# Weight preparations of the gate stage: one tile to load into and another to store from, sums made in place, and a new timetable

## The chip, the cores and the metric

The kernel runs on one core of a Trainium2 chip. The metric is device time in microseconds (us) of the whole program, so lower is better. Engines are named as the profile names them: PE is TensorE's matmul and PEld its weight load, DVE is VectorE, ACT is ScalarE, POOL is GpSimd, SP is SyncE, which does nothing here but issue DMAs. Each engine works through its own queue in order, and an instruction that waits holds what stands behind it on that queue.

## The reference, cut to what matters

The input is layer-normalised; a Fourier mixing layer and a gated feed-forward layer work on the same normalised x, and both are added to the residual.

```python
xn = _layernorm(x)                                   # x: 2048 x 640
a  = einsum("bsd,ed->bse", xn, dft_hid_re)
b  = einsum("bsd,ed->bse", xn, dft_hid_im)
yA = einsum("ts,bse->bte", dft_seq_re, a) - einsum("ts,bse->bte", dft_seq_im, b)
gate = einsum("bsd,df->bsf", xn, W_gate)             # 640 x 1728
up   = einsum("bsd,df->bsf", xn, W_up)
h    = gate * (gate > 0) * up
yB   = einsum("bsf,fd->bsd", h, W_down)              # 1728 x 640
return x + yA + yB
```

The kernel orders the matrix products another way (the sequence transform of xn first, then the product with the hidden matrices together with W_down) and writes them as Winograd-like block products: sums and differences of blocks stand in for some of the multiplications. Each fp32 product is three matmuls of rounded high and low parts, which the helper `mm3` issues on lines 205 to 207.

## The kernel before, in words

There are three stages. The first streams the sequence matrix and normalises x. The second, the **gate stage**, makes the gate and up products for 13 tiles of 128 columns. The third, `project`, multiplies everything by the hidden matrices and W_down.

The gate stage has a timetable written out by hand. Every action is filed under a key with `at(key, function)`; the list is sorted by key, and the instructions of all engines are issued in that order. A tile takes `PERIOD = 33` keys. In a whole-numbered key stands one block product, which is three matmuls on PE; other work has fractional keys between them. `STEPS` holds the products (`mm`), the copies that seed a new PSUM bank from an old one (`seed`, line 1094, on ACT), snapshots (`snap`, line 196) and sums (`add`, line 1104; `addout`, line 1109; both on DVE). `SUMS` lists differences of weight blocks on line 999, which `plan_sums` puts on DVE or on POOL by their due keys. `WEIGHTS` are the roundings of weights to high parts on ACT (line 196) and low parts on DVE (line 1075).

Beside the gate products, the stage also prepares weights that the third stage needs. There are 29 **preparations**, numbered here from 0: five of `quad_weights`, then 24 of `pair_half`. Three stand in each tile from the third tile on, at the keys in `TASK_KEYS`. A preparation has five steps, each filed under its own key:

- `load`, `TASK_LEAD` keys ahead: two DMAs on SP's queue (line 1256 or 1292) into a tile `pw`
- `prepare`: three or four sums of 128x128 blocks on DVE (lines 1263 to 1266, or 1298 and on with the helper on line 625)
- `round_`, 1.2 keys later: one rounding on ACT (line 1270 or 1305)
- `rounded`, at the second number of the pair in `TASK_KEYS`: the low part on DVE (line 1274 or 1309)
- `store`, `TASK_STORE` keys after that: one or two DMAs on SP (lines 1278 and 1280, or 1312) to the DRAM tensors `wparts` or `wquads`

The pool `prep` has two buffers, each 12 blocks wide. A `pw` tile holds what is loaded, what is computed and what is stored, so the load of preparation i writes into the tile of preparation i-2 and waits on SP until the store of i-2 has landed. SP's queue also carries the results of the gate products (`hd`, line 1130) and the next tile's raw weights (lines 986, 991, 996). POOL's queue has DMAs of its own, the sums of data for the third stage (`grown`, lines 1338 and 1339) and unchanged weight blocks (line 1241).

`rest_weights` takes a tile of the same pool ahead of the gate stage, and `lead_unit` takes some at its end.

Of the kernel before, what the change touches and what calls it, by code (L numbers as in the profile page):

```python
# [127 lines left out]
def fnet_reglu_kernel(  # L128
# [877 lines left out]
    def plan_sums():  # L1006

        split_at = {b: key for key, src, first, k, _ in WEIGHTS if src == "z" for b in range(first, first + k)}
        reads = {}
        for i, (_, o, _, a, b) in enumerate(SUMS):  # L1010
            for x in (a, b):
                reads.setdefault(x, []).append(i)
        made = {o: i for i, (_, o, *_) in enumerate(SUMS)}
        due = {}

        def due_at(i):
            if i not in due:
                o = SUMS[i][1]
                raw = max(SUMS[i][3:]) >= ZR
                due[i] = min([split_at.get(o, 99.0) - 9, RAW_DUE if raw else 99.0] + [due_at(j) - 0.8 for j in reads.get(o, ())])  # L1020
# [133 lines left out]
    def rest_weights():  # L1154
        st = stage()[:, :D]
        nc.sync.dma_start(st, wrest)
        rest["w"] = w = pool("prep").tile([P, 12 * P], F32R, name="pw")[:, : 2 * D].rearrange("p (v d) -> p v d", v=2)
        split(w[:, 0], w[:, 1], st)

    def rest_block(i, k):  # L1160
        ks = sorted(range(KD), key=lambda k: block(k, CHUNKS[i]) in late_raw)
        return block(ks[k], CHUNKS[i])

    def rest_multiply(i, k):
        d = rest_block(i, k) // NT
        w, cs = rest["w"], slice(d * P, (d + 1) * P)
        if k == 0:
            rest[i] = new_bank()
        mm3(rest[i], (w[:, 0, cs], w[:, 1, cs]), place[rest_block(i, k)], k == 0, k == KD - 1)
# [74 lines left out]
    def pair_half(k, h):  # L1244

        t = {}
        z1, z4, y11, y12, y21 = (slice(i * P, (i + 1) * P) for i in range(5))
        hi, lo = slice(5 * P, 8 * P), slice(8 * P, 11 * P)
        z2, z3, y22 = (slice(i * P, (i + 1) * P) for i in (8, 9, 10))

        def load():
            t["z"] = z = pool("prep").tile([P, 12 * P], F32, name="pw")
            wa, wb = pair(k, 1)
            blocks = z.rearrange("p (o n) -> p o n", n=P)
            for w, put in ((wa[0], slice(2, 5, 2)), (wb[0], slice(3, 11, 7))):
                nc.sync.dma_start(blocks[: w.shape[0], put], w.rearrange("p (o n) -> p o n", n=P)[:, h : h + 4 : 3])

        def prepare():
            z = t["z"]
            if k == ODD:  # L1260
                nc.vector.memset(z[REST:, y12], 0.0)
                nc.vector.memset(z[REST:, y22], 0.0)
            tt(z[:, z1], z[:, y21], z[:, y22], op=OP.add)
            blocks = z.rearrange("p (o n) -> p o n", n=P)
            tt(blocks[:, 8:10], blocks[:, 0:3:2], blocks[:, 2:5:2], op=OP.subtract)
            tt(z[:, z4], z[:, y12], z[:, z2], op=OP.subtract)

        def round_():
            z = t["z"]
            nc.scalar.activation(z[:, hi].bitcast(F32R), z[:, lo], AF.Copy)  # L1270

        def rounded():
            z = t["z"]
            tt(z[:, lo], z[:, lo], z[:, hi], op=OP.subtract)

        def store():
            z = t["z"]
            nc.sync.dma_start(wparts[:, k, : 10 * P].rearrange("p (a n) -> p a n", a=2)[:, :, h * P : (h + 1) * P],
                                z[:, : 2 * P].rearrange("p (a n) -> p a n", a=2))
            nc.sync.dma_start(wparts[:, k, HIGH:NW].rearrange("p (v n) -> p v n", n=2 * P)[:, :, h * P : (h + 1) * P],  # L1280
                                z[:, 5 * P : 11 * P].rearrange("p (v n) -> p v n", n=P))

        return load, prepare, round_, rounded, store

    def quad_weights(i):

        t = {}

        def load():
            t["z"] = z = pool("prep").tile([P, 12 * P], F32, name="pw")  # L1290
            for j, k in enumerate(QUADS[i]):
                nc.sync.dma_start(z[:, j * 2 * P : (j + 1) * 2 * P], pair(k, 1)[1][0][:, : 2 * P])

        def prepare():
            a11, a21, a12, a22 = (t["z"][:, j * P : (j + 1) * P] for j in range(4))
            t["s"] = s = t["z"][:, 4 * P : 12 * P].rearrange("p (s v n) -> p s v n", s=4, v=2)
            s1, s2, s3, s4 = (s[:, j, 1] for j in range(4))
            tt(s1, a22, a21, op=OP.subtract)
            minus(s2, s1, a11)
            tt(s3, a11, a21, op=OP.subtract)  # L1300
            minus(s4, a12, s2)

        def round_():
            s = t["s"]
            nc.scalar.activation(s[:, :, 0].bitcast(F32R), s[:, :, 1], AF.Copy)

        def rounded():
            s = t["s"]
            tt(s[:, :, 1], s[:, :, 1], s[:, :, 0], op=OP.subtract)

        def store():
            nc.sync.dma_start(wquads[:, i], t["s"].rearrange("p s v n -> p s (v n)"))

        return load, prepare, round_, rounded, store
# [33 lines left out]
    def lead_unit(u):  # L1348
# [439 lines left out]
```

## Time and profile before

| | us |
|---|---|
| median of 3 runs | 1016.29 |
| lowest and highest run | 1012.73, 1021.4 |
| the profiled execution's own time | 1020.64 |
| its span, first to last instruction | 1018.8 |
| PE busy | 999.3 (98%) |
| DVE busy | 882.7 (87%) |
| ACT busy | 525.0 (52%) |
| POOL busy | 146.0 (14%) |

The profiled execution is one run by itself. Its time is 1.84 us more than its span, and 4.35 us above the median of the three timed runs. The gate stage lies from about 398 to 740 us of the span. Waits are read as "engine, instruction, releaser: us in total, times, longest"; in a timeline the first two numbers are an instruction's start and duration, and the bracket at the end is the idle time of its engine ahead of it and what ended that.

### The profile page before, as it was taken

Reading aid. Unit: us, or ns where it says so; the run is one execution under the profiler, and the core shown is the slowest. Engines: PE = TensorE matmul, PEld = TensorE weight load, DVE = VectorE, ACT = ScalarE, POOL = GpSimd, SP = SyncE. Lnnn points to the kernel's source line nnn. Section 1 sums busy time; section 2 is a strip of 40 time slices with the busy share of each in tenths; the row PEclk is TensorE's granted clock in tenths of the full one; section 3 lists DMA queues with packets and bytes.
Section 4 is the critical chain, followed back from the end, with each engine's and each line's share of the span. In section 5 each row is a group of like instructions: output and inputs, shape, how many; then the busy total and the mean of one; then the engine's idle time right before and its main releaser. Section 6 shows DMA issues by size and latency. Waiting matters only on the chain.

```text
span 1018.8 us, 13540 instructions
## 1 busy us (share of the span) xinstructions
PE 999.3 (98%) x4393; PEld 820.8 (81%) x4393; DVE 882.7 (87%) x1440; ACT 525.0 (52%) x832; POOL 146.0 (14%) x285
## 2 busy tenths in 40 slices
PE   9999999999999999999899899999999999999998
PEld 7888888888888888778688678888877888888887
DVE  7968999999989989989799689997778888589877
ACT  6664443433333556776476466666434454444542
POOL 2000000000000000034344344432000001000001
PEclk9999999999999999999899989999999999999999
DMA  9877894977939867547687888866599779999785
GB/s 333 328 231 278 265 341 141 388 266 233 374 126 333 297 216 267 196 133 196 211 259 225 232 230 237 220 195 177 183 388 322 228 249 330 317 300 341 223 259 184
DMA packets 183669, 261.12 MB, mean 256 GB/s; under 512 B 14944, under 2 KB 127200, under 8 KB 183504
## 3 DMA queue, kind: packets, MB, share of 16 engines
q1 hardware_dynamic: 147200, 208.82, 60.7%
q0 software_dynamic: 10944, 38.44, 12.9%
q10 hardware_dynamic: 25456, 13.01, 4.3%
q8 instruction: 34, 0.56, 0.2%
q14 instruction: 35, 0.29, 0.1%
HBM read 198.34 MB, written 75.94 MB: 269 GB/s over the span
## 4 chain that ended last, share of the span: by engine, by line
PE 84%; DMA 6%; DVE 6%; ACT 2%; issue 1%; SPq 0%; POOL 0%; DVEq 0%; ACTq 0%
PE ps L205 26%; PE ps L206 26%; PE ps L207 26%; PE ps L583 3%; DMA wparts<-pw 2%; DMA wquads<-pw 1%; DMA rw<-pq 1%; DVE gw L999 1%; PE ps L612 1%; DMA pw<-in_wd 1%; DMA rw<-hd 1%; DVE w L1075 1%; DMA wt<-wparts 1%; PE ps L1587 1%; DVE ev L1109 1%
## 5 line engine op out<-in xcount | busy, mean ns | idle before, releaser
L206 PE MATMUL ps<-cb,wt 128*128 128x512 f32 (+1 forms) x389 | 151.5, 390 | 1.3 <-DVE cb L200 1.2
L205 PE MATMUL ps<-cb,wt 128*128 128x512 f32 (+1 forms) x389 | 151.1, 388 | 0.4 <-ACT cb L199 0.4
L207 PE MATMUL ps<-cb,wt 128*128 128x512 f32 (+1 forms) x389 | 150.9, 388 | 0.0
L199 ACT ACTIVATE cb<-rw 128x1024 fp32r<-128x1024 f32 (+1 forms) x91 | 86.6, 962 | 77.4 <-PE ps L207 39.8
L199 ACT ACTIVATE cb<-raw 128x1024 fp32r<-128x1024 f32 x64 | 67.7, 1060 | 103.3 <-PE ps L207 70.8
L200 DVE TENSOR_TENSOR cb<-rw,cb 128x1024 fp32r<-128x1024 f32 (+1 forms) x91 | 99.4, 1103 | 18.2 <-ACT cb L199 17.6
L206 PE MATMUL ps<-cb,xs_late 128*128 128x512 f32 x232 | 90.5, 390 | 0.0
L207 PE MATMUL ps<-cb,xs_late 128*128 128x512 f32 x232 | 90.3, 389 | 0.0
L205 PE MATMUL ps<-cb,xs_late 128*128 128x512 f32 x232 | 90.3, 389 | 0.0
L196 ACT ACTIVATE ev<-ps 128x512 f32<-128x512 f32 x117 | 69.7, 596 | 38.3 <-PE ps L207 36.4
L200 DVE TENSOR_TENSOR cb<-raw,cb 128x1024 fp32r<-128x1024 f32 x64 | 77.9, 1218 | 13.1 <-ACT cb L199 13.0
L1094 ACT ACTIVATE ps<-ps 128x512 f32<-128x512 f32 x104 | 59.3, 582 | 58.0 <-DVE ps L1104 36.9
L206 PE MATMUL ps<-cb,xs_early 128*128 128x512 f32 x226 | 88.0, 390 | 0.0
L205 PE MATMUL ps<-cb,xs_early 128*128 128x512 f32 x226 | 87.9, 389 | 0.0
L207 PE MATMUL ps<-cb,xs_early 128*128 128x512 f32 x226 | 87.9, 389 | 0.0
L206 PEld LDWEIGHTS ps<-cb,wt 128*128 128x128 f32 x389 | 73.0, 188 | 18.3 <-DVE cb L200 3.3
L205 PEld LDWEIGHTS ps<-cb,wt 128*128 128x128 f32 x389 | 73.0, 188 | 15.8 <-ACT cb L199 0.8
L207 PEld LDWEIGHTS ps<-cb,wt 128*128 128x128 f32 x389 | 73.0, 188 | 14.9
L1109 DVE TENSOR_TENSOR ev<-ps,ev 128x512 f32<-128x512 f32 x91 | 62.4, 686 | 13.0 <-PE ps L207 12.0
L199 ACT ACTIVATE wt<-wt 128x768 fp32r<-128x768 f32 (+5 forms) x60 | 38.4, 646 | 56.6 <-DMA wt<-wparts 54.9
L999 POOL TENSOR_TENSOR gw<-gw 128x128 f32<-128x128 f32 x99 | 45.9, 463 | 149.6 <-DVE gw L999 62.2
L205 PE MATMUL ps<-mv,w 128*128 128x512 f32 x143 | 57.1, 399 | 5.6 <-ACT ps L1094 5.6
(250 smaller groups left out, 2290.4 us busy)
## 6 DMA issues: line engine op xcount, KB each, us to landing
raw<-in_dft SPq DMA_DIRECT2D x94, 512.0 KB, 6.5
wt<-wparts SPq DMA_DIRECT2D x74, 256.0 KB, 4.9
rw<-hd SPq DMA_DIRECT2D x27, 512.0 KB, 6.7
hd<-ev SPq DMA_DIRECT2D x45, 256.0 KB, 3.1
tok<-r ACTq DMA_DIRECT2D x24, 448.0 KB, 6.0
wt<-wparts SPq DMA_DIRECT2D x27, 384.0 KB, 5.0
rw<-pq SPq DMA_DIRECT2D x19, 512.0 KB, 5.8
wparts<-pw SPq DMA_DIRECT2D x24, 384.0 KB, 4.2
```

What stands on the lines that cost most here:

```text
L196: return nc.scalar.activation(o, i, AF.Copy)
L199: nc.scalar.activation(hi, src, AF.Copy)
L200: return nc.vector.tensor_tensor(lo, src, hi.bitcast(F32), op=OP.subtract)
L205: nc.tensor.matmul(ps, wh, mh, start=first, stop=False, skip_group_check=more)
L206: nc.tensor.matmul(ps, wh, ml, start=False, stop=False, skip_group_check=more)
L207: nc.tensor.matmul(ps, wl, mh, start=False, stop=last, skip_group_check=more)
L583: nc.tensor.matmul(E[0, key], xn_part(n * SG + j, d)[v == 1], b[:, int(v == 2), j], start=False, stop=n % NH == NH - 1 and (j, v) == (SG - ...
L612: nc.tensor.matmul(E[c, key], xn_part(j, d)[v == 1], b[c][0][:, int(v == 2), j], start=j == 0 and v == 0, stop=False)
L999: return (engine or nc.vector).tensor_tensor(operand(n, o), operand(n, a), operand(n, b), op=OP.add if op == "+" else OP.subtract)
L1075: tt(w[:, 1, : k * P], operand(n, first, k), w[:, 0, : k * P].bitcast(F32), op=OP.subtract)
L1094: nc.scalar.activation(banks[n, x], banks[n, s], AF.Copy, scale=float(sign))
L1109: tt(t, banks[n, x], snaps[n, s], op=OP.add if op == "+" else OP.subtract)
```

## The change

Each preparation now has two tiles. `pl`, four blocks wide, takes the load; `pw`, now eight blocks wide, is what the store reads. Both have two buffers, so the pool's size stays 24 blocks. The load of preparation i now waits until preparation i-2 has read its `pl` for the last time (in `rounded` for a pair, in `prepare` for a quad), not until its store has landed. The first sum of preparation i writes into `pw`, and so waits for the store of i-2.

Two of the sums of a pair are written over the loaded blocks. One sum of 256 columns becomes two of 128, so a pair has four sums instead of three; for the odd pair two clears become one. The rounding reads `pl` and writes `pw`. In `wparts` the order of three block columns changes, and what the third stage reads follows it by the constants `Y22, Z2, Z3`.

The timetable moves as well: loads 13.0 keys ahead (11.1 before), stores 2.8 keys after the last sum (2.0 before), the middle preparation of a tile two keys later, the first fourteen roundings of token sums two keys earlier (`FIRST_SPLIT`), and the due keys of the weight sums one key later. `rest_weights` takes two tiles instead of one.

```diff
-SPLIT_LEAD, FIRST_SPLIT = 5.5, -16
-TASK_STORE = 2.0
-TASK_LEAD, TASK_KEYS = 11.1, ((8.2, 12.4), (16.6, 20.4), (31.2, 33.1))
+SPLIT_LEAD, FIRST_SPLIT = 5.5, -18
+TASK_STORE = 2.8
+TASK_LEAD, TASK_KEYS = 13.0, ((8.2, 12.4), (18.6, 22.4), (31.2, 33.1))
-Z2, Z3, Y22 = (2 * P * i for i in range(3))
+Y22, Z2, Z3 = (2 * P * i for i in range(3))
...
-                due[i] = min([split_at.get(o, 99.0) - 9, RAW_DUE if raw else 99.0] + ...
+                due[i] = min([split_at.get(o, 99.0) - 8, RAW_DUE if raw else 99.0] + ...
...
     def rest_weights():
-        rest["w"] = w = pool("prep").tile([P, 12 * P], F32R, name="pw")[:, : 2 * D].rearrange("p (v d) -> p v d", v=2)
-        split(w[:, 0], w[:, 1], st)
+        rest["w"] = w = [pool("prep").tile([P, 8 * P], F32R, name="pw")[:, :D] for _ in range(2)]
+        split(w[0], w[1], st)
...
     def pair_half(k, h):
-        z1, z4, y11, y12, y21 = (slice(i * P, (i + 1) * P) for i in range(5))
-        hi, lo = slice(5 * P, 8 * P), slice(8 * P, 11 * P)
-        z2, z3, y22 = (slice(i * P, (i + 1) * P) for i in (8, 9, 10))
+        z1, z4, hi, lo = slice(0, P), slice(P, 2 * P), slice(2 * P, 5 * P), slice(5 * P, 8 * P)
         def load():
-            t["z"] = z = pool("prep").tile([P, 12 * P], F32, name="pw")
+            t["y"] = y = pool("prep").tile([P, 4 * P], F32, name="pl")
...
         def prepare():
-            z = t["z"]
+            y = t["y"]
+            y12, y22, y11, y21 = (y[:, i * P : (i + 1) * P] for i in range(4))
+            t["z"] = z = pool("prep").tile([P, 8 * P], F32, name="pw")
             if k == ODD:
-                nc.vector.memset(z[REST:, y12], 0.0)
-                nc.vector.memset(z[REST:, y22], 0.0)
-            tt(z[:, z1], z[:, y21], z[:, y22], op=OP.add)
-            blocks = z.rearrange("p (o n) -> p o n", n=P)
-            tt(blocks[:, 8:10], blocks[:, 0:3:2], blocks[:, 2:5:2], op=OP.subtract)
-            tt(z[:, z4], z[:, y12], z[:, z2], op=OP.subtract)
+                nc.vector.memset(y[REST:, : 2 * P], 0.0)
+            tt(z[:, z1], y21, y22, op=OP.add)
+            tt(y21, y11, y21, op=OP.subtract)
+            tt(y11, z[:, z1], y11, op=OP.subtract)
+            tt(z[:, z4], y12, y11, op=OP.subtract)
         def round_():
-            nc.scalar.activation(z[:, hi].bitcast(F32R), z[:, lo], AF.Copy)
+            nc.scalar.activation(t["z"][:, hi].bitcast(F32R), t["y"][:, P:], AF.Copy)
         def rounded():
-            tt(z[:, lo], z[:, lo], z[:, hi], op=OP.subtract)
+            tt(z[:, lo], t["y"][:, P:], z[:, hi], op=OP.subtract)
...
     def quad_weights(i):
         def load():
-            t["z"] = z = pool("prep").tile([P, 12 * P], F32, name="pw")
+            t["y"] = z = pool("prep").tile([P, 4 * P], F32, name="pl")
         def prepare():
-            t["s"] = s = t["z"][:, 4 * P : 12 * P].rearrange("p (s v n) -> p s v n", s=4, v=2)
+            t["s"] = s = pool("prep").tile([P, 8 * P], F32, name="pw").rearrange("p (s v n) -> p s v n", s=4, v=2)
...
     def lead_unit(u):
-            z = pool("prep").tile([P, 12 * P], F32, name="pw")
+            z = pool("prep").tile([P, 8 * P], F32, name="pw")
```

PE's order of instructions does not change anywhere. On the other engines the moves are these.

SP's queue around preparation 15, the first that loads from W_down and the first preparation of its tile, before the change. Its loads are the two rows with `in_wd`, the store of preparation 13 is the two rows with `wparts` above them; the brackets name the semaphores that a row waits for, `DMAHW` for DMAs that SP issued.

```order
L1278 DMA wparts<-pw 128x2x128 [waits DMAHW3_49,DVE_49]
L1280 DMA wparts<-pw 128x6x128 [waits DMAHW4_49,DVE_49,Activation_49]
L1130 DMA hd_92<-ev_4936 128x512 [waits DMAHW5_49,DVE_49]
L1130 DMA hd_92<-ev_4832 128x512 [waits DVE_49]
L1256 DMA pw<-in_wd 128x2x128 [waits DMAHW4_49,DMAHW3_49]
L1256 DMA pw<-in_wd 128x2x128 [waits DMAHW0_49]
```

The same place after the change.

```order
L1276 DMA wparts<-pw 128x2x128 [waits DMAHW3_49,DVE_49]
L1278 DMA wparts<-pw 128x6x128 [waits DMAHW4_49,DVE_49]
L1130 DMA hd_92<-ev_4958 128x512 [waits DMAHW5_49,DVE_49]
L1130 DMA hd_92<-ev_4852 128x512 [waits DMAHW6_49,DVE_49]
L1253 DMA pl<-in_wd 128x2x128 [waits DMAHW7_49]
L1253 DMA pl<-in_wd 128x2x128 [waits DMAHW0_49]
```

The rows stand in the same order. What has gone is the first load's wait for semaphores 3 and 4, which the two halves of the store above it raise. What is left is the wait for the DMA that used the row's own semaphore eight DMAs earlier.

ACT's queue around preparation 4, the last quad and the middle preparation of its tile, before the change. Line 1305 is the preparation's rounding, `ev<-ps` on line 196 a snapshot, `ps<-ps` on line 1094 a seed of a bank, `w<-gw` a high part of a weight.

```order
L196 ACTIVATE w_4231<-gw 128x384 [waits Pool_49]
L196 ACTIVATE ev_4250<-ps 128x512 [waits DVE_49,PE_49]
L1305 ACTIVATE pw<-pw 128x4x128 [waits DMAHW7_49,DMAHW0_49,DVE_49]
L196 ACTIVATE ev_4256<-ps 128x512 [waits PE_49]
L1094 ACTIVATE ps<-ps 128x512 [waits PE_49,Activation_49]
L1094 ACTIVATE ps<-ps 128x512 [waits DVE_49]
L196 ACTIVATE w_4300<-gw 128x384 [waits Pool_49]
```

And after.

```order
L196 ACTIVATE w_4235<-gw 128x384 [waits Pool_49]
L196 ACTIVATE ev_4250<-ps 128x512 [waits DVE_49,PE_49]
L196 ACTIVATE ev_4258<-ps 128x512 [waits DVE_49,PE_49]
L1094 ACTIVATE ps<-ps 128x512 [waits PE_49,Activation_49]
L1303 ACTIVATE pw<-pw 128x4x128 [waits DMAHW7_49,DVE_49]
L1094 ACTIVATE ps<-ps 128x512 [waits DVE_49]
L196 ACTIVATE w_4302<-gw 128x384 [waits Pool_49]
```

The rounding, which waits for the preparation's sums on DVE, has moved from ahead of the second snapshot to behind the first of the two seeds. It does so in the middle preparation of every tile; the first and the last preparation of a tile keep their places on ACT. On DVE, in the same place, one low part of a weight (line 1075) now stands ahead of the preparation's sums, and the preparation's own low part (line 1309) has moved behind two sums into PSUM (line 1104) and one out of it (line 1109).

More of the change, by code (lines that the diff above doesn't have):

```diff
@@ L1019, in due_at @@
                 raw = max(SUMS[i][3:]) >= ZR
-                due[i] = min([split_at.get(o, 99.0) - 9, RAW_DUE if raw else 99.0] + [due_at(j) - 0.8 for j in reads.get(o, ())])
+                due[i] = min([split_at.get(o, 99.0) - 8, RAW_DUE if raw else 99.0] + [due_at(j) - 0.8 for j in reads.get(o, ())])
             return due[i]
@@ L1168, in rest_multiply @@
             rest[i] = new_bank()
-        mm3(rest[i], (w[:, 0, cs], w[:, 1, cs]), place[rest_block(i, k)], k == 0, k == KD - 1)
+        mm3(rest[i], (w[0][:, cs], w[1][:, cs]), place[rest_block(i, k)], k == 0, k == KD - 1)
     def rest_read(i):
@@ L1246, in pair_half @@
         t = {}
-        z1, z4, y11, y12, y21 = (slice(i * P, (i + 1) * P) for i in range(5))
-        hi, lo = slice(5 * P, 8 * P), slice(8 * P, 11 * P)
-        z2, z3, y22 = (slice(i * P, (i + 1) * P) for i in (8, 9, 10))
+        z1, z4, hi, lo = slice(0, P), slice(P, 2 * P), slice(2 * P, 5 * P), slice(5 * P, 8 * P)
         def load():
-            t["z"] = z = pool("prep").tile([P, 12 * P], F32, name="pw")
+            t["y"] = y = pool("prep").tile([P, 4 * P], F32, name="pl")
             wa, wb = pair(k, 1)
-            blocks = z.rearrange("p (o n) -> p o n", n=P)
-            for w, put in ((wa[0], slice(2, 5, 2)), (wb[0], slice(3, 11, 7))):
-                nc.sync.dma_start(blocks[: w.shape[0], put], w.rearrange("p (o n) -> p o n", n=P)[:, h : h + 4 : 3])
+            for w, at in ((wa[0], 2), (wb[0], 0)):
+                nc.sync.dma_start(y[: w.shape[0], at * P : (at + 2) * P].rearrange("p (o n) -> p o n", n=P),
+                                    w.rearrange("p (o n) -> p o n", n=P)[:, h : h + 4 : 3])
         def prepare():
-            z = t["z"]
+            y = t["y"]
+            y12, y22, y11, y21 = (y[:, i * P : (i + 1) * P] for i in range(4))
+            t["z"] = z = pool("prep").tile([P, 8 * P], F32, name="pw")
             if k == ODD:
-                nc.vector.memset(z[REST:, y12], 0.0)
-                nc.vector.memset(z[REST:, y22], 0.0)
[L1263 to L1266, printed above, removed]
+                nc.vector.memset(y[REST:, : 2 * P], 0.0)
[3 more added lines that the diff above has]
+            tt(z[:, z4], y12, y11, op=OP.subtract)
         def round_():
-            z = t["z"]
-            nc.scalar.activation(z[:, hi].bitcast(F32R), z[:, lo], AF.Copy)
+            nc.scalar.activation(t["z"][:, hi].bitcast(F32R), t["y"][:, P:], AF.Copy)
         def rounded():
             z = t["z"]
-            tt(z[:, lo], z[:, lo], z[:, hi], op=OP.subtract)
+            tt(z[:, lo], t["y"][:, P:], z[:, hi], op=OP.subtract)
         def store():
@@ L1280, in store @@
             nc.sync.dma_start(wparts[:, k, HIGH:NW].rearrange("p (v n) -> p v n", n=2 * P)[:, :, h * P : (h + 1) * P],
-                                z[:, 5 * P : 11 * P].rearrange("p (v n) -> p v n", n=P))
+                                z[:, 2 * P :].rearrange("p (v n) -> p v n", n=P))
         return load, prepare, round_, rounded, store
@@ L1294, in prepare @@
         def prepare():
-            a11, a21, a12, a22 = (t["z"][:, j * P : (j + 1) * P] for j in range(4))
-            t["s"] = s = t["z"][:, 4 * P : 12 * P].rearrange("p (s v n) -> p s v n", s=4, v=2)
+            a11, a21, a12, a22 = (t["y"][:, j * P : (j + 1) * P] for j in range(4))
+            t["s"] = s = pool("prep").tile([P, 8 * P], F32, name="pw").rearrange("p (s v n) -> p s v n", s=4, v=2)
             s1, s2, s3, s4 = (s[:, j, 1] for j in range(4))
```

## The prediction

> **What bounds the kernel now.** I read the page's first line, then what PE waited for in the gate stage, then that stage in slices, then the order of events at the two places where slices fall short.
>
> ```profile
> span 1018.8 us, 13540 instructions
> ```
>
> ```profile
> PE ps L205 <- ACT ps L1094: 11.1, 3, 5.6
> PE ps L205 <- ACT ev L196: 1.0, 1, 1.0
> ```
>
> The second fence is PE's waits from 398 to 740 us. PE waits for seeds of PSUM banks three times, 11.1 us in all. The slices say where; the columns are busy times of PE, PEld, DVE, ACT and POOL with their counts, then the granted clock, the DMA engines' busy share and GB/s.
>
> ```profile
> 470.00:482.00 12.00, 12.00 (x55) 9.93 (x54) 11.90 (x30) 7.16 (x15) 7.04 (x13) 1.00 0.94 222
> 482.00:494.00 12.00, 8.74 (x39) 6.92 (x37) 6.32 (x15) 5.24 (x11) 2.83 (x6) 0.97 0.71 220
> 494.00:506.00 12.00, 10.52 (x37) 8.55 (x38) 10.52 (x25) 6.08 (x13) 5.81 (x12) 0.75 0.64 203
> 506.00:518.00 12.00, 12.00 (x55) 9.93 (x54) 10.14 (x23) 8.47 (x17) 4.62 (x10) 1.00 0.81 224
> ...
> 566.00:578.00 12.00, 12.00 (x55) 9.93 (x54) 11.22 (x24) 6.43 (x15) 7.26 (x14) 1.00 0.96 223
> 578.00:590.00 12.00, 6.36 (x23) 4.85 (x22) 4.86 (x12) 4.56 (x10) 1.86 (x4) 0.81 0.74 252
> 590.00:602.00 12.00, 12.00 (x50) 9.80 (x49) 9.83 (x25) 5.55 (x12) 4.96 (x10) 0.91 0.77 192
> ...
> sum 348.00, PE 335.14 PEld 273.03 DVE 299.39 ACT 216.95 POOL 114.83; mean PE 11.56 PEld 9.41 DVE 10.32 ACT 7.48 POOL 3.96
> ```
>
> PE is full nearly everywhere: the stage is bound by PE, except around 490 and 581 us, where every engine goes idle together and the clock falls (0.75 and 0.81). Just before each the DMA engines are 0.94 and 0.96 busy. The timeline of the first place:
>
> ```profile
> 478.49 0.33 SPq L1312 DMA_DIRECT2D wquads<-pw  x1
> 488.33 0.81 SPq L1292 DMA_DIRECT2D pw<-in_wd  x2
> ...
> 488.54 0.39 PE L205 MATMUL ps<-mv,wa 128*128 128x512 f32 x1
> ...
> 490.36 0.39 PE L207 MATMUL ps<-r,wb 128*128 128x512 f32 x1
> ...
> 492.77 0.29 DVE L1298 TENSOR_TENSOR pw<-pw 128x128 f32<-128x128 f32 x1 [4.69 <-DMA pw<-in_wd]
> ...
> 493.82 0.63 ACT L1305 ACTIVATE pw<-pw 128x512 fp32r<-128x512 f32 x1 [5.16 <-DVE pw L625]
> ...
> 494.83 0.59 ACT L1094 ACTIVATE ps<-ps 128x512 f32<-128x512 f32 x1
> ...
> 495.48 0.80 PE L205 MATMUL ps<-xs_early,wa 128*128 128x512 f32 x1 [4.73 <-ACT ps L1094]
> ...
> 500.19 0.39 PE L207 MATMUL ps<-mv,wa 128*128 128x512 f32 x1
> ```
>
> Read it upwards. PE stands because a seed on ACT is late; the seed stands behind a preparation's rounding (line 1305); that waits for sums on DVE (line 1298), and these for the load of preparation 4, issued only at 488.33. The second place:
>
> ```profile
> 569.74 0.89 SPq L1256 DMA_DIRECT2D pw<-in_hid  x2
> ...
> 571.25 0.41 SPq L1280 DMA_DIRECT2D wparts<-pw  x1
> ...
> 580.34 2.57 SPq L1256 DMA_DIRECT2D pw<-in_wd  x2
> ...
> 581.13 0.39 PE L207 MATMUL ps<-mv,w 128*128 128x512 f32 x1
> ...
> 584.70 0.29 DVE L1263 TENSOR_TENSOR pw<-pw 128x128 f32<-128x128 f32 x1 [6.75 <-DMA pw<-in_wd]
> 585.03 0.42 DVE L1265 TENSOR_TENSOR pw<-pw 128x256 f32<-128x256 f32 x1
> ...
> 585.49 0.29 DVE L1266 TENSOR_TENSOR pw<-pw 128x128 f32<-128x128 f32 x1
> 585.70 0.28 DVE L999 TENSOR_TENSOR gw<-st,gw 128x128 f32<-128x128 f32 x1
> ...
> 587.16 0.79 PE L205 MATMUL ps<-mv,w 128*128 128x512 f32 x1 [5.64 <-ACT ps L1094]
> ...
> 592.32 0.40 PE L205 MATMUL ps<-mv,w 128*128 128x512 f32 x1
> ```
>
> It is the same chain with preparation 15. What held the two loads on SP, from the chain that ended last, SP's waits and the list of DMA issues:
>
> ```profile
> 478.49 9.78 DMA wquads<-pw
> ...
> 571.25 9.04 DMA wparts<-pw
> ```
>
> ```profile
> SPq L1256 <- DMA wparts<-pw: 68.4, 23, 7.5
> ```
>
> ```profile
> wparts<-pw SPq DMA_DIRECT2D x24, 384.0 KB, 4.2
> ```
>
> The stores of preparations 2 and 13 took 9.78 and 9.04 us against a median of 4.2, and the loads behind them were issued as soon as they had landed. SP stood 68.4 us in 23 such waits; only two of all preparations were late enough to stop PE.
>
> **Price of the two stalls.** Matmuls start every (490.36 - 488.54) / 8 = 0.2275 us. In the first stall, 495.48 - 490.36 - 0.2275 = 4.89 us pass without one. Then eleven steps, to 500.19, take 4.71 us instead of 2.50: 2.21 lost to the lower clock. In the second, 587.16 - 581.13 - 0.2275 = 5.80, then twelve steps in 5.16 instead of 2.73: 2.43. In all 7.10 + 8.23 = **15.33 us**.
>
> [...]
>
> **The change, part by part.**
>
> *Loads no longer wait for stores: both stalls go.* A key is three matmuls, 3 x 0.2275 = 0.68 us. Before, a store was due 2.3 to 5.3 us ahead of the load that waited for it (for preparations 2 and 4: from key 33.1 + 2.0 to key 33 + 16.6 - 11.1, 3.4 keys). A store of 9 us breaks that. Now the load waits for a read of `pl` that is due 5.5 to 5.8 keys (3.7 us) earlier, and is issued 13 keys, 8.9 us, ahead of its use.
>
> *A new wait takes its place.* DVE's first sum writes the `pw` tile of i-2 and waits for that store. Due times: from key 33.1 + 2.8 to 33 + 18.6, 22.4 + 2.8 to 33 + 8.2, 12.4 + 2.8 to 31.2; that is 15.7 to 16 keys, 10.7 to 10.9 us. Queued behind the wait on DVE are the sums into PSUM banks, and behind those the seeds and PE. Both long stores fit. Preparation 4: DVE was ready at 492.77 - 4.69 = 488.08; two keys later is 489.45. Its store, 0.8 keys later than at 478.49, lands at 479.04 + 9.78 = 488.82: 0.6 us to spare. Preparation 15: DVE was ready at 584.70 - 6.75 = 577.95. The store of 13 was due 16 keys before, at 567.03, and sat behind the load at 569.74, which is free now; at 9.04 us it lands at 576.07: 1.9 us to spare. What is late next is nothing that I can see; the margins are thin.
>
> *DVE's extra sum.* In the second place the three sums take 585.70 - 584.70 = 1.00 us to the next start, and a 128-wide one followed by one that needs it takes 0.33. Four sums, three of them waiting for the one ahead and the last followed by free work at 585.70 - 585.49 = 0.21, take 3 x 0.33 + 0.21 = 1.20 at most. If the in-place ones overlap as free work does, 0.33 + 3 x 0.21 = 0.96. So -0.04 to +0.20 us for a pair, -1.0 to +4.8 us over 24 pairs. The stage's DVE is busy 299.39 of 348 us, and PE was full in a slice where DVE had 11.90 of 12; I take nothing on the path, and 4.8 as the bound if that cover is gone.
>
> *Moved work.* On ACT the middle preparation's rounding falls behind the first seed, so a late load there stops the seed no more: a gain in cases that I already count as gone, so nothing. The next tile's raw weights fall behind two loads on SP: issuing takes 0.89 us (row at 569.74), and they are asked for more than a tile ahead (`LOAD_LEAD` 46 keys); nothing. Weight sums due one key later lose 0.68 us of a lead of 9 keys; nothing, 0.68 x 11 tiles = 7.5 us if every tile were tight. The roundings that move two keys earlier are at the start of the stage, where DVE works without a pause and the same work comes in another order: between losing and gaining that place's largest wait, 1.0 us (second fence); I take 0.
>
> **The sum.** 1020.64 - 15.33 = 1005.31 for an execution like the profiled one. That one lies 4.35 us over the median of 1016.29. The lowest run, 1012.73, is 7.91 below it, about what one stall costs (7.10 or 8.23), so I infer that the runs differ mostly in how much of these stalls they had, and that all come down to the same floor: **1005 us**. If instead the spread has other causes, the median loses the full sum: 1016.29 - 15.33 = 1001.0.
>
> **The rivals.**
>
> - *One stall comes back, on the store.* The two places are those where the DMA engines are 0.94 and 0.96 busy; a store that lands 2 us later than before misses DVE at both. Loads issued earlier add traffic just there. [...] Against it: stores are no longer issued in clumps after a blocked load. With 3 us of wait at one place up to a whole stall: 1005.3 + 3 to 1005.3 + 8.2, so 1008 to 1013.5. Chance 0.24.
> - *The profiled execution had stalls that the usual run has not.* Then the change removes what is rarely there, and the time stays near the lowest run, 1012 to 1016. Against it: the median lies nearer to the profiled run than to a run without stalls. Chance 0.10.
> - *Slower: every preparation's store ends behind its use, and the wait is now on DVE instead of SP.* SP's 68.4 us of waits cost nothing by themselves; on DVE each stops the banks. It decides where stores take over 10.9 us as a rule: at 12 us, 24 x 1.1 = 26 us, so 1031; it eats up the gain from 15.33 / 24 = 0.64 us over, 11.5 us a store. The median of 4.2 speaks against it. Chance 0.08.
>
> **How the numbers follow.** Both stalls gone: 0.58, with its own range from 1001.0 (spread of other causes) to 1005.3 + 4.8 = 1010 (DVE's bound). With the first two rivals 0.92 is covered by 1001 to 1016; cutting the upper ends of the rivals and leaving a little below for the wait at the start, I give 1000 to 1014. About 1% is what a measurement of this kernel can tell from no change, here 1006.1 to 1026.5. Of the first case I put four fifths below 1006.1: 0.47, with a little from a short wait of the first rival 0.48. Slower is the last rival, 0.08; the rest is 0.44.
>
> **What would show it.** Right: PE's waits for seeds on line 1094 fall from 11.1 us to about 1; the clock is 1.00 in all slices from 446 to 720 us; SP's waits of loads for `wparts` and `wquads` stores vanish; DVE's first sum waits under 1 us for any DMA. First rival: a DVE wait of 2 us or more on a `wparts` or `wquads` store with an idle PE behind it. Slower: such waits on most preparations. Wrong in the size: stalls gone, and PE's idle time found elsewhere, in the low parts on line 1075 (late weight sums) or at the start of the stage. A time above 1010 with no wait on a preparation would say that the stalls were not what the runs lost.

## The result, and the profile after

| | before | after |
|---|---|---|
| median, measured side by side (8 runs each) | 1021.65 us | 1008.03 us |
| lowest and highest run | 1012.73, 1024.01 | 1006.75, 1009.38 |
| the profiled execution's own time | 1020.64 | 1008.12 |
| its span | 1018.8 | 1006.3 |
| its mean granted clock | 0.993 | 1.000 |

The ratio is 0.9886, with a 95% interval from 0.9856 to 0.9915: the change makes the kernel 1.1% faster. The prediction's 1005 us is 3.0 us too low, inside its range. The eight runs of before have their median 5.4 us above that of the three shown earlier, which are among them.

The page of after, its first line, busy times and granted clock in 40 slices:

```profile
span 1006.3 us, 13555 instructions
...
PE 994.3 (99%) x4393; PEld 816.8 (81%) x4393; DVE 884.8 (88%) x1462; ACT 526.1 (52%) x832; POOL 146.1 (15%) x285
...
PEclk9999999999999999999999999999999999999999
```

PE's waits in after, from 398 to 740 us, and below them SP's four longest rows, all ended by a DVE result, then DVE's waits for DMAs in the preparations (us in total, times, longest):

```profile
PE ps L205 <- ACT ev L196: 1.4, 1, 1.4
PE ps L205 <- ACT ps L1094: 1.2, 3, 0.7
PE ps L205 <- DVE ps L1115: 0.6, 2, 0.3
```

```profile
SPq L1130 <- DVE ev L1121: 58.4, 29, 4.9
SPq L1278 <- DVE pw L1272: 38.5, 16, 2.8
SPq L1276 <- DVE gw L999: 23.9, 12, 5.2
SPq L1310 <- DVE pw L1307: 18.2, 5, 5.7
```

```profile
DVE pw L1296 <- DMA pl<-in_wd: 0.7, 1, 0.7
DVE pw L1262 <- DMA pl<-in_wd: 0.5, 1, 0.5
```

PE's waits for seeds (line 1094) have fallen from 11.1 us to 1.2. No load of a preparation waits for a store any more. Before, there were the 68.4 us of the prediction and two rows that it does not name, 2.0 us and this one, which is the load of preparation 4 and so the first stall:

```profile
SPq L1292 <- DMA wquads<-pw: 9.5, 1, 9.5
```

SP now stands ahead of its own stores and results until DVE has made them. No wait of DVE for a store is listed.

The slices of after around the two places of the stalls:

```profile
482.00:494.00 12.00, 12.00 (x55) 9.93 (x54) 10.07 (x28) 9.35 (x19) 4.32 (x9) 1.00 0.94 297
494.00:506.00 12.00, 11.65 (x52) 9.29 (x51) 11.83 (x27) 6.71 (x14) 5.63 (x11) 1.00 0.75 213
...
566.00:578.00 12.00, 12.00 (x54) 9.95 (x53) 11.54 (x26) 8.96 (x18) 6.23 (x13) 1.00 0.96 242
578.00:590.00 12.00, 12.00 (x54) 9.87 (x53) 11.24 (x29) 6.85 (x15) 6.05 (x12) 1.00 0.86 219
```

The clock is 1.00 in all four, and the DMA engines are as busy as before (0.94 and 0.96). How preparation 4 now passes, from the chain of waits (first fence: start, us, what), the timeline of after, and the times from issue to landing of the five `wquads` stores (line 1310):

```profile
480.62 10.03 DMA pl<-in_wd
...
499.21 0.59 ACT ps L1094
...
499.85 0.50 PE ps L205
```

```profile
479.75 0.33 SPq L1310 DMA_DIRECT2D wquads<-pw  x1
480.13 0.91 SPq L1290 DMA_DIRECT2D pl<-in_wd  x2
...
490.73 0.29 DVE L1296 TENSOR_TENSOR pw<-pl 128x128 f32<-128x128 f32 x1 [0.72 <-DMA pl<-in_wd]
490.75 0.58 ACT L1094 ACTIVATE ps<-ps 128x512 f32<-128x512 f32 x1
...
491.78 0.63 ACT L1303 ACTIVATE pw<-pw 128x512 fp32r<-128x512 f32 x1 [0.45 <-DVE pw L625]
...
492.53 0.39 PE L205 MATMUL ps<-mv,w 128*128 128x512 f32 x1
```

```profile
DMA to landing us min/median/max: 2.7/4.9/10.3
```

The load goes out at 480.13 instead of 488.33. In this crowded stretch it takes 10.03 us, longer than its lead of 8.9, and DVE waits 0.72 us for it. PE does not stop here: the seed at 490.75 now stands ahead of the rounding at 491.78. But the delay comes out later. DVE goes on with hardly a pause, and the same chain leads 9 us on to a late seed (499.21) and a stop of PE of 0.51 us, 0.62 with the slower step behind it. In eight profiles (four of the change, four of kernels below that differ little from it at this place) DVE is late here by 0.04, 0.33, 0.50, 0.66, 0.72, 0.80, 0.87 and 1.38 us, and the stop of PE some 9 us later is 0, 0.12, 0.28, 0.45, 0.51, 0.58, 0.66 and 0.97.

The store of preparation 2, for which the same first sum of DVE waits, went out at 479.75 and is the one that took 10.3 us. It landed at 490.09, and DVE had been free since 490.73 - 0.72 = 490.01. No list shows this, because a wait is put down to what came last, and the load landed at 490.65.

**Where the time went.** From one profile to the other, 12.52 us went. I add up how far the starts of consecutive matmuls lie apart beyond 0.2275 us. In the gate stage that is 20.02 us before and 6.18 after, so 13.84 less. From 446 us on it is 16.47 and 1.62; of the 16.47 the two stalls are 15.33. Against the forecast of 15.33 us these are missing: 1.00 at the start of the stage, where 4.55 us are lost instead of 3.55 (three more profiles of the same kernel lose 3.48, 3.73 and 3.9 there, so most of it differs from execution to execution); 0.48 in short stops (0.62 at 499 us and 0.44 at 679, where before loses 0.58 beside its two stalls); 0.33 in steps too short for my count; 0.31 in the first stage, 0.25 in the third, 0.43 behind the last matmul. Together that is 2.80, and 15.33 - 2.80 = 12.53.

### The profile page after: what moved, and what is told of

It is laid out like the page before. It is cut to its first block, busy times and chain, and to the rows that moved or that the text cites. A ratio compares the mean times of both kernels' runs of the same rounds, so it can differ in the third digit from the quotient of the medians.

```text
span 1006.3 us, 13555 instructions
## 1 busy us (share of the span) xinstructions
PE 994.3 (99%) x4393; PEld 816.8 (81%) x4393; DVE 884.8 (88%) x1462; ACT 526.1 (52%) x832; POOL 146.1 (15%) x285
## 4 chain that ended last, share of the span: by engine, by line
PE 72%; DVE 11%; issue 8%; DMA 6%; ACT 2%; SPq 1%; POOL 0%; DVEq 0%; ACTq 0%; POOLq 0%
PE ps L205 23%; PE ps L206 23%; PE ps L207 23%; PE ps L583 3%; DVE cb L200 2%; DVE raw L750 1%; DMA pq<-sb 1%; DMA pl<-in_wd 1%; DVE gw L999 1%; DMA rw<-pq 1%; DMA pq<-sa 1%; PE ps L612 1%; DMA rw<-hd 1%; DVE w L1075 1%; PE ps L1585 1%
## 5 line engine op out<-in xcount | busy, mean ns | idle before, releaser
L999 POOL TENSOR_TENSOR gw<-gw 128x128 f32<-128x128 f32 x104 | 48.5, 467 | 134.3 <-DVE gw L999 55.1
L199 ACT ACTIVATE cb<-tk 128x1024 fp32r<-128x1024 f32 x32 | 33.8, 1060 | 50.1 <-DVE tk L750 24.5
```

The lines of the kernel that those rows point to most:

```text
L999: return (engine or nc.vector).tensor_tensor(operand(n, o), operand(n, a), operand(n, b), op=OP.add if op == "+" else OP.subtract)
```

## The experiments

Kernels of one set ran on one chip, beside runs of the kernel before on it. Ratios are against those.

### First set: which part carries it (before: 1022.63 us)

**The new tiles with all the old times.**

```diff
-SPLIT_LEAD, FIRST_SPLIT = 5.5, -18
-TASK_STORE = 2.8
-TASK_LEAD, TASK_KEYS = 13.0, ((8.2, 12.4), (18.6, 22.4), (31.2, 33.1))
+SPLIT_LEAD, FIRST_SPLIT = 5.5, -16
+TASK_STORE = 2.0
+TASK_LEAD, TASK_KEYS = 11.1, ((8.2, 12.4), (16.6, 20.4), (31.2, 33.1))
...
-                due[i] = min([split_at.get(o, 99.0) - 8, ...
+                due[i] = min([split_at.get(o, 99.0) - 9, ...
```

> Two tiles, with every number of the old timetable (loads 11.1 keys ahead, stores 2.0 keys after the last sum, middle preparation at 16.6, first roundings at -16, sums due at -9). Theory (the load's wait for a landed store makes the stalls, so the tiles carry the gain): a store now has from 14.5 keys (9.9 us, middle preparation) to 18.8 keys (12.8 us) to land; both stalls go, PE waits under 2 us for seeds in the gate stage, time within 3 us of the change's, 1005 to 1010. Rival (the timetable carries the gain, the tiles alone only move the wait to the first sum): at least one stall with a lower clock stays, 1012 or more.

1008.78 us, ratio 0.9872 (0.9823 to 0.9922). PE's longest row of waits for seeds, from 395 to 760 us:

```profile
PE ps L205 <- ACT ps L1094: 1.0, 2, 0.7
```

The stalls are gone without the new timetable. The tiles carry the gain. The sums made in place come with the tiles; no run separates the two.

**The old tile with all the new times.** The reverse: the kernel before, with one tile of twelve blocks and the sums as they were, and the change's numbers in the timetable. The edit is against the kernel before.

```diff
-SPLIT_LEAD, FIRST_SPLIT = 5.5, -16
-TASK_STORE = 2.0
-TASK_LEAD, TASK_KEYS = 11.1, ((8.2, 12.4), (16.6, 20.4), (31.2, 33.1))
+SPLIT_LEAD, FIRST_SPLIT = 5.5, -18
+TASK_STORE = 2.8
+TASK_LEAD, TASK_KEYS = 13.0, ((8.2, 12.4), (18.6, 22.4), (31.2, 33.1))
...
-                due[i] = min([split_at.get(o, 99.0) - 9, ...
+                due[i] = min([split_at.get(o, 99.0) - 8, ...
```

> One tile of 12 blocks as before, with every number of the new timetable. Theory: the load still waits for the store of two before, which is now due only 2.7 to 3.0 keys (2 us) ahead of it; SP waits for wparts and wquads stores 60 us or more, a store of 9 to 10 us still makes the load land after its use; stalls of PE stay, 1015 to 1025. Rival (timetable): the stalls shrink or go, 1012 or less.

1024.26 us, ratio 1.0021 (0.9989 to 1.0052): no gain. Waits from 395 to 760 us, of SP, DVE and PE, in a profiled execution of 1032.65 us, well above that median:

```profile
SPq L1256 <- DMA wparts<-pw: 112.8, 25, 9.1
...
SPq L1292 <- DMA wquads<-pw: 15.5, 3, 10.0
```

```profile
DVE pw L1263 <- DMA pw<-in_hid: 12.0, 3, 7.4
DVE pw L1263 <- DMA pw<-in_wd: 10.3, 5, 7.1
```

```profile
PE ps L205 <- ACT ps L1094: 16.8, 6, 6.4
```

Loads that are due earlier only stand longer behind the stores, 112.8 us instead of 68.4, and in this execution PE waits for six seeds instead of three. An earlier time for a load was worth nothing here (ratio 1.0021) while its tile wasn't free.

**Stores 9 keys behind the last sum.** This tests the first rival: the change with its window for the store shortened by 6.2 keys, 4.2 us.

```diff
-TASK_STORE = 2.8
+TASK_STORE = 9.0
```

> The change with stores 9.0 keys after the last sum instead of 2.8, so a store has 9.5 to 9.8 keys (6.5 us) until the first sum two preparations on, instead of 10.7 us. Theory (only stores longer than this window matter): the usual store of 4 us costs nothing; those of 7 to 10 us at two to four places make DVE wait 1 to 3 us each for wparts or wquads; 3 to 9 us slower than the change, 1011 to 1017. Rival (stores were never near the limit, the margins worked out are far too thin): within 1.5 us of the change. Rival (every store is near the limit): 1025 or more.

1011.12 us, ratio 0.9901 (0.9874 to 0.9928), and 1015.8 in the profiled execution. Its timeline where it lost most, then its slices there:

```profile
522.61 0.47 SPq L1278 DMA_DIRECT2D wparts<-pw  x1
...
532.13 0.29 DVE L1262 TENSOR_TENSOR pw<-pl 128x128 f32<-128x128 f32 x1 [3.18 <-DMA wparts<-pw]
532.19 0.39 PE L207 MATMUL ps<-mv,w 128*128 128x512 f32 x1
532.46 0.29 DVE L1263 TENSOR_TENSOR pl<-pl 128x128 f32<-128x128 f32 x1
...
534.78 0.79 PE L205 MATMUL ps<-mv,w 128*128 128x512 f32 x1 [2.21 <-ACT ps L1094]
...
535.38 0.63 PE L206 MATMUL ps<-mv,w 128*128 128x512 f32 x1
...
535.80 0.63 PE L207 MATMUL ps<-mv,w 128*128 128x512 f32 x1
```

```profile
532.00:536.00 4.00, 1.79 (x6) 1.18 (x5) 3.76 (x11) 2.09 (x4) 0.46 (x1) 0.84 0.47 143
536.00:540.00 4.00, 4.00 (x15) 3.17 (x14) 2.33 (x5) 1.91 (x4) 2.52 (x5) 0.74 0.52 128
```

The store at 522.61 lands 9.4 us later, DVE waits 3.18 us for it, the seed is late, PE stops, and the clock falls. DVE waits once more for a `wparts` store, 2.3 us, and twice for a `wquads` store, some 0.5 each. So the rival's mechanism is real, and it is the length of the window that keeps it small: with 2.8 keys no such wait is listed, though the store of preparation 2 comes as late as the load beside it.

**The middle preparation back at its old keys.**

```diff
-TASK_LEAD, TASK_KEYS = 13.0, ((8.2, 12.4), (18.6, 22.4), (31.2, 33.1))
+TASK_LEAD, TASK_KEYS = 13.0, ((8.2, 12.4), (16.6, 20.4), (31.2, 33.1))
```

> The change with the middle preparation back at keys 16.6 and 20.4, so its store window falls from 15.7 to 13.7 keys (9.3 us) and its rounding on ACT goes back ahead of the seed. Theory: at preparation 4 a store or load of 9 to 10 us makes DVE late by up to 1.5 us with the seed behind it; 0 to 3 us slower than the change, 1007 to 1011. Rival (the moved middle preparation carries the gain): a stall of 4 us or more with a lower clock returns, 1013 or more.

1010.81 us, ratio 0.9888 (0.9842 to 0.9934). There is no long stall, but there are short stops: 0.83 us at 492, 0.61 at 675, and one of 0.13 us, with a first step 0.11 us too long behind it, in each of the seven tiles from 516 to 653 us. These seven stand at the middle preparation, where the rounding is back ahead of the seed. By the matmuls' starts 4.48 us are lost from 446 to 700 us, against 1.1 to 1.6 in four profiles of the change. It was not timed beside the change itself, and its ratio is the change's. But its four runs, 1010.57 to 1011.22, all lie above the 26 runs of the change on other chips, 1006.60 to 1009.38. So the old keys of the middle preparation cost about 3 us here, inside the theory's range, as far as runs on different chips can say.

### Second set: what the timetable is worth (before: 1020.58 us)

Four kernels: the change again, the new tiles with all the old times again (the same edit as in the first set), the change with `FIRST_SPLIT` back at -16, and that with loads 16 keys ahead.

> The changed kernel itself, for comparison on one chip with the next three. Theory: 1006 to 1010, no long stop of PE in the gate stage.

> The two tiles with the old timetable once more, beside the change on the same chip. If the timetable is worth anything by itself, this is at least 1 us slower than the change (its store windows are 9.9 to 12.8 us, uneven, instead of 10.7 to 10.9); if the tiles carry everything, within 1 us.

```diff
-SPLIT_LEAD, FIRST_SPLIT = 5.5, -18
+SPLIT_LEAD, FIRST_SPLIT = 5.5, -16
```

> The change with the first fourteen roundings back at -16. In the change's profile PE loses 1.0 us more than before at the start of the stage (398 to 446 us), and ACT waits 3.7 us there for token sums to land. Theory (the earlier roundings meet loads that have not landed): the wait goes, 0.3 to 1 us faster than the change. Rival (that loss comes from how the first stage ended in this execution): same within 0.3 us.

```diff
-TASK_LEAD, TASK_KEYS = 13.0, ((8.2, 12.4), (18.6, 22.4), (31.2, 33.1))
+TASK_LEAD, TASK_KEYS = 16.0, ((8.2, 12.4), (18.6, 22.4), (31.2, 33.1))
```

> The run before with loads 16 keys ahead instead of 13 (10.9 us instead of 8.9). In the change's profile the load of preparation 4 took 10.03 us and DVE waited 0.7 us for it. Theory: that wait goes, and with it PE's 0.4 us stop behind it; 0 to 1 us faster than the run before. Rival (the load then waits for the last read of its tile, due only 2.5 keys ahead of it, and holds SP): slower by 1 us or more, SP waits of loads for DVE.

| | median of 6 | lowest, highest | ratio, 95% |
|---|---|---|---|
| the change | 1007.72 | 1006.95, 1008.39 | 0.9881 (0.9841 to 0.9921) |
| new tiles, old times | 1009.12 | 1008.77, 1010.15 | 0.9898 (0.9862 to 0.9934) |
| `FIRST_SPLIT` back | 1007.31 | 1006.30, 1011.67 | 0.9885 (0.9847 to 0.9923) |
| and loads 16 keys ahead | 1007.90 | 1006.66, 1008.64 | 0.9884 (0.9848 to 0.9920) |

The timetable as a whole is worth 1.4 us, and the runs of the two kernels do not overlap. The 3 us above are for the middle preparation moved back alone; why that costs more than all the old times together no run shows. The profile with the old times has a stop of 0.95 us at 493, behind preparation 4: there the rounding still stands ahead of the seed. The profile of that kernel in the first set has no such stop, so it comes with some executions.

My theory that the earlier roundings cost the 1 us at the start of the stage is not borne out. Without them ACT's wait for token sums is gone, but the stage's start still loses 3.9 and 4.3 us in the last two kernels' profiles, against 3.5 to 4.6 in the change's, and the medians lie 0.41 us below and 0.18 above the change's, with runs that overlap: no difference is shown.

A longer lead brings the load of preparation 4 in on time, and gains nothing clear either. DVE's first sum is still late, by 0.50 us instead of 0.72 to 1.38:

```profile
490.88 0.29 DVE L1296 TENSOR_TENSOR pw<-pl 128x128 f32<-128x128 f32 x1 [0.50 <-issue]
```

The view does not say what ended this wait. The store of preparation 2 does: it went out at 480.89, behind the load now, and landed 9.9 us later, at 490.80, 2.6 us after the load. So taking away the load's delay brings out the first rival's wait behind it, and PE still stops for 0.28 us, at 500 us. A new wait appears too, of SP on the read of the tile that the load goes into:

```profile
SPq L1253 <- DVE pw L1272: 26.7, 7, 5.8
```

### Third set: what a sum on DVE costs (before: 1017.64 us)

The first sum of each pair is made twice, with the same result: 24 more sums of 0.33 us from start to start, 7.9 us on DVE. Beside it runs the change.

```diff
             tt(z[:, z1], y21, y22, op=OP.add)
+            tt(z[:, z1], y21, y22, op=OP.add)
```

> The change with the first sum of every pair made twice: 24 more sums of 128x128 on DVE, 0.33 us each to the next start, 7.9 us in all; each repeats a sum that is there already, so nothing else changes. Theory (the fourth sum of a pair lies beside PE's work and costs nothing): within 1 us of the change on the same chip. Rival (DVE is on the path in the gate stage, so the change paid for its extra sum): 3 to 8 us slower than the change.

> The changed kernel itself, beside the run before on the same chip: 1006 to 1010.

1012.18 us (0.9937, 0.9913 to 0.9960) against 1007.68 (0.9891, 0.9857 to 0.9926): 4.5 us slower. Theory and measurement part here: I had held DVE's sums to be free. One tile's length, in the change first (the profile of the result) and then with the sum added:

```profile
536.00:558.50 22.50, 22.50 (x101) 18.61 (x100) 21.18 (x52) 14.99 (x31) 10.84 (x21) 1.00 0.82 250
```

```profile
536.00:558.50 22.50, 22.50 (x99) 18.17 (x98) 21.73 (x54) 14.50 (x31) 9.95 (x21) 1.00 0.79 241
```

PE is "busy" for 22.50 us in both, because a matmul's record of 0.39 us overlaps the next, which starts 0.2275 us later. The counts differ: 101 and 99. The waits of PE's weight loads show why, again the change of the result first, both from 398 to 740 us:

```profile
PEld ps L205 <- ACT ps L1094: 3.4, 6, 1.1
PEld ps L205 <- DVE ps L1115: 1.6, 3, 0.7
```

```profile
PEld ps L205 <- ACT ps L1094: 7.2, 15, 1.1
PEld ps L205 <- DVE ps L1115: 3.9, 10, 0.7
```

Seeds and sums into banks come a little late at 25 places instead of 9. Most of the new ones cost PE some 0.2 us each, too little to be listed as a wait of PE. By the matmuls' starts the gate stage loses 9.84 us with the sum added and 5.49 in the profile of the change beside it: 4.35 us more, close to the 4.5 between the medians.

### Fourth set: a sum taken off DVE (before: 1022.91 us)

```diff
-            tt(z[:, z4], y12, y11, op=OP.subtract)
+            nc.gpsimd.tensor_tensor(z[:, z4], y12, y11, op=OP.subtract)
```

> The change with the fourth sum of each of the 24 pairs (line 1265) made by POOL instead of DVE; nothing else moves. Theory A: beside e12, 24 sums more on DVE cost 4.5 us because seeds stand behind sums on a DVE that is busy 21.2 of 22.5 us a tile; so the change's own fourth sum, which came with the in-place form, costs something too, and taking it off gives back 1 to 3 us: 1005 to 1007. Theory B: at the change's load PE already loses only some 1.5 us between 446 and 700 us, so there is next to nothing to win, and the fourth sum did cost nothing: within 1 us of the change beside it. Against both: POOL takes about 0.47 to 0.51 us for such a sum and stands in waits for DVE, so the first store of a pair or a sum into weights behind it may come late: over 1 us slower than the change.

> The change as it is, beside the run before it on the same chip: 1007 to 1008.5 us, as in its other runs.

1007.39 us (0.9857, 0.9830 to 0.9884) against 1007.50 (0.9856, 0.9831 to 0.9881): the same. But it does not show that the fourth sum is free, because DVE was not relieved. Eight tile lengths from 446 to 626 us, busy time of each engine, then DVE's weight sums in that stretch, in the change of the result:

```profile
sum 180.00, PE 179.65 PEld 148.09 DVE 166.88 ACT 119.01 POOL 82.29; mean PE 22.46 PEld 18.51 DVE 20.86 ACT 14.88 POOL 10.29
```

```profile
L999 DVE TENSOR_TENSOR gw<-gw 128x128 f32<-128x128 f32 x47 | 12.0, 285 | 0.0
L1265 DVE TENSOR_TENSOR pw<-pl 128x128 f32<-128x128 f32 x17 | 5.0, 292 | 0.6
```

And with the sum on POOL (line 1265 is a row of POOL, from 446 to 700 us):

```profile
sum 180.00, PE 179.91 PEld 148.32 DVE 166.98 ACT 118.96 POOL 90.31; mean PE 22.49 PEld 18.54 DVE 20.87 ACT 14.87 POOL 11.29
```

```profile
L999 DVE TENSOR_TENSOR gw<-gw 128x128 f32<-128x128 f32 x47 | 14.0, 328 | 0.0
```

```profile
L1265 POOL TENSOR_TENSOR pw<-pl 128x128 f32<-128x128 f32 x24 | 11.3, 470 | 30.6 <-DVE pl L1264 19.8 <-ACT ev L196 5.0 <-DMA pl<-in_wd 2.9
```

DVE has 17 sums, 5.0 us, less in this stretch and is as busy as before, since other work takes longer: the same 47 weight sums take 328 ns instead of 285. The mean hides two kinds. Of all 75 weight sums in the stretch, 12 take 527 ns, and each of these runs beside a sum on POOL; the other 63 take 283. Not every sum beside POOL is slowed, as 21 of the 63 quick ones overlap a sum there too, and no run shows what sets the 12 apart.

Not tried: three buffers of the old tile, which might also have freed the loads. A third buffer is 6 KB in each partition (12 x 128 x 4 bytes); whether it fits beside this kernel's other pools no run shows.

## Why the prediction was right, and where it was off

**The two stalls: right, in cause and nearly in size.** The first step said that both came from loads held on SP by stores, and priced them at 15.33 us. With separate tiles they are gone, with the old times too; with the old tile they stay, with the new times too. The gate stage lost 13.84 us less. Of the 1.49 us that are missing, 1.00 is at the start of the stage, where executions differ, and 0.48 in short stops, of which the one at 499 us comes from the change's own transfers (below). Among SP's waits the prediction lists only those for `wparts`; the stall at preparation 4 is in the row for `wquads`, 9.5 us.

**The starting point and the inference on the runs: half right.** I took the three runs' median as typical and the profiled execution as 4.35 us over it. The profiled execution was the typical one: the eight-run median is 1021.65, which speaks against the second rival. My inference was that the runs of before differ mostly in how much of the stalls they had. Over 56 runs of before in the four sets the time follows the granted clock (correlation 0.81, some 1.5 us for each 0.001 of the mean clock), from 1010.11 us at 1.000 to 1028.35 at 0.992. Over 26 runs of the change it goes from 1006.60 to 1009.38 only. What did not hold is the common floor: the line through the runs of before meets a full clock at 1013 us, 5 us above the change's median of 1007.8. My estimate, from the single stops of 1.53 and 1.57 us that left the clock alone (last section), is that such executions still have a few stops of that size; no profile shows one.

**The new wait on DVE: right that it comes in place of the old one, wrong in its margins.** The prediction had 0.6 and 1.9 us to spare at the two places, and called them thin. At preparation 15 the store of 13 took 3.0 us, not 9.04, and 7.1 were to spare. At preparation 4 none was. DVE was ready at 490.01, the store went out at 479.75 instead of 479.04, took 10.3 us instead of 9.78, and landed 0.1 us too late; in the other three profiles of the change it took 10.5 to 11.0 us and landed 0.2 to 0.7 too late. That this cost next to nothing by itself is luck: the load landed later still. Taking 4.2 us of the window away brings the wait out (3.18 us) and costs 2.3 us against the new tiles with the old times in the same set (1011.12 and 1008.78): the first rival's mechanism, a little below its lower price of 3, with runs of the two kernels that overlap.

**"What is late next is nothing that I can see": wrong, at a price of about 0.5 us.** The load of preparation 4 was late next, since it took 10.03 us with a lead of 8.9. DVE's 0.72 us behind it became PE's 0.51 at 499 us.

**Moved work: under-sized by 1.4 us.** I counted ACT's moved rounding at nothing, as a gain only where a stall was already counted as gone. The timetable as a whole gains 1.4 us. What the runs show in place of nothing is the rounding ahead of the seed: a stop of 0.95 us at preparation 4 with the old times, and with the middle preparation alone moved back a short stop in seven tiles, 4.48 us lost in all against 1.1 to 1.6. The prediction saw a gain only where a load is late; the rounding also waits for sums that are on time. For `FIRST_SPLIT`, taken at 0, no difference is shown (1007.31 against 1007.72).

**DVE's extra sum: nothing on the path holds, its reason does not.** Its length is the upper bound that I gave: in the timeline above, the in-place sums start 0.33 us apart. My cover was that PE had been full in a slice with DVE at 11.90 of 12 us. Adding another such sum shows that cover to be thin: 7.9 us more on DVE cost 4.5. That slice had PE's busy time full, which says little, as the counts of 101 and 99 show. The run with the fourth sum on POOL did not relieve DVE, but the matmuls' starts say more. From 446 to 700 us the change's four profiles lose 1.06 to 1.62 us, of which the stop at 499 us, ahead of the first pair's sums, is 0.62 to 1.08. The 0.43 to 0.54 that is left is no more than the 15.91 - 15.33 = 0.58 that the kernel before loses there beside its two stalls. So no price of the fourth sum is seen in this stretch. That it is free where one sum more is not was luck as far as the prediction's reason goes; why the limit lies just there stays open.

**The slower rival** needed stores of over 10.9 us as a rule. In the change's profiles one store of a preparation comes near that or over it, that of preparation 2 with 10.3 to 11.0 us; the medians are 4.2 us for `wparts` and 4.9 for `wquads`.

## What to carry to other kernels

When a load waits for a store of two steps ago, look for the tile that they share: a small tile for what is loaded and another for what is stored frees the load within the same space (here SP's 68.4 us of waits for `wparts` went), where an earlier issue time alone only lengthens the wait (here to 112.8 us). Put an instruction that may wait for a transfer behind the copy that PE needs, not ahead of it (here 4.48 us were lost with the middle preparation's rounding ahead, against 1.1 to 1.6). Judge whether an engine has time to spare by the number of matmuls in a stretch and by the waits of the weight loads, not by PE's busy share (22.50 us here with 101 matmuls and with 99), and test it by adding one instruction (7.9 us of sums cost 4.5). A wait is put down to what came last: look when the other things landed before you call a transfer harmless, and follow a small delay of an engine without pauses to the next stop.

## What the runs showed of the hardware

**After a stop of 2.4 us PE's steps went from 0.2275 to 0.42 us.** With stores 9 keys late PE had no matmul from 532.42 (532.19 + 0.2275) to 534.78, 2.36 us, and then went at steps of 0.42 us (535.38 to 535.80), at a granted clock of 0.74 from 536 to 540 us. After the two stalls of before, 4.89 and 5.80 us, the steps were 0.42 to 0.43 us behind a first one of 0.59, at a granted clock of 0.50 (495 to 500 and 588 to 592 us). Single stops of 1.53 us in the profile of the result (425.51 to 427.04) and of 1.57 us with one more sum (427.09 to 428.66) left the clock alone: one step of 0.34 us, then steps of 0.22 to 0.24. Two short stops together did not: in the profile of the change in the third set, stops of 1.36 and 1.03 us with one matmul between them (745.9 to 748.5 us) were soon followed by eight steps of 0.41 to 0.43 us, and the granted clock fell to 0.63:

```profile
750.00:754.00 4.00, 4.00 (x13) 3.17 (x12) 3.73 (x4) 2.27 (x4) 0.00 (x0) 0.63 1.07 393
```

In the profile of the result the same two stops were 1.18 and 1.03 us, and the clock stayed at 1.00. So a stop of 2.4 us has to be priced with its restart, which cost 1.7 us here, and 2.2 and 2.4 after the two stalls of before.

**Landing times spread widely.** Loads of 128 KB from `in_wd` landed 5.0 us after their issue in the median, and one took 10.03 where the DMA engines were 0.94 busy; beside it a store of 512 KB took 10.3, with a median of 4.9. A lead worked out from the median would have been half of what was needed.
